# Moving work in the opening of a hash-attention and SwiGLU kernel: a turn, a bit copy, squares and zeros

## Chip, cores and metric

The kernel runs on one core of one Trainium2 chip. The metric is the device time of one execution in microseconds (us); the engines are named as the profile names them: PE (matmul; PEld is its weight load), DVE (vector), ACT (scalar), POOL (GpSimd) and SP (which here only issues DMAs).

## What is computed

First an attention with hashed buckets, over 4 batches, 8 heads, 768 tokens and a head size of 64; then a gated feed-forward layer on its output.

```python
q_bits = (einsum('bhsd,dk->bhsk', q, proj) > 0)        # 6 bits; k_bits likewise
mask = q_bucket[..., :, None] == k_bucket[..., None, :]
scores = where(mask, q @ k.T / 8, -1e9)
attn = softmax(scores);  x = (attn @ v)                 # [3072, 512] after the heads are joined
xn = x / sqrt(mean(x * x) + 1e-6) * rms_g
out = (silu(xn @ w_gate) * (xn @ w_val)) @ w_out        # 512 -> 1536 -> 512
```

## The kernel before

**The tiles.** A unit of work `w` is half a batch (384 queries), so there are eight. A pair `(b, hp)` is two heads of a batch. The six buffers `QK0` to `QK5` (line 95) each hold the turned keys and queries of one pair in fp16: rows 0 to 63 the 64 columns of the head, rows 64 to 75 twelve rows of hash bits, so that one matmul over the rows gives the score and a penalty for unequal bits. Pairs are given buffers in turn: (0,0) to (0,3) get QK0 to QK3, (1,0) and (1,1) get QK4 and QK5, (1,2) and (1,3) get QK0 and QK1 again. `score_rows` (line 141) says how many rows a score matmul reads: 76, or all 128 where rows 76 to 127 have been cleared by `clear_rows` (line 138), which the opening does on POOL for QK4 and QK5.

**The slots.** The program is written in a fixed order by hand. Each of the 192 slots (`SLOTS`, line 36) makes the scores of one head and a third of the keys (two PE matmuls of 384 columns, line 355) and one exponential on ACT (line 365). Score tiles have two buffers, so the scores of a slot wait for the exponential of two slots before. In slot `s` the scores of slot `s+1` are issued first; then the work planned for the slot with `at(s, f, ...)`, in order of rank, is issued to all engines. Every engine works its own queue in that order. So a wait of one instruction holds all that stands behind it on the same engine.

**From a load to a score in the first pairs.** SP loads a pair's `kL`, `qL`. PE turns a head (three transposes, line 181) into a bank `t_ps`; DVE copies it out to fp32 `kT` or `qT` (line 189); POOL, and ACT for a quarter, cast it into QK rows 0 to 63 (lines 195 and 197). A hash matmul on PE (line 221, bank `d_ps`) and a comparison on DVE (line 228) give `bits`. These lie on other partitions than the QK rows 64 to 75, so twelve rows at a time are moved: blocks 0 and 1 of each head by DVE copies (lines 261 and 281) and the odd blocks 2 and 3 by SP's DMA (lines 259 and 279). Slot 1 of a head of unit 0 reads block 2.

**After the scores.** `av` multiplies the exponentials with the values (line 377, one accumulator bank `o_ps`). DVE adds a small constant (`otmp`, line 392) and takes the reciprocal (397); POOL multiplies them into `x` (404) and makes its squares `sq` (416), and DVE sums these into `ssp` (420). For the pairs (0,2) and (0,3), which are called urgent, DVE does the product and squares with a running sum itself (404, 411). `norm` sums `ssp` to `ss` (427) and POOL makes `rstd` (429, 433). DVE scales `x` to `xn` (444), PE turns it (458, `x_ps`), DVE copies it to `xnT` (459), and the gate and value matmuls read that (473, 483). For unit 0 these turns stand in slots 38 to 40 and the first gate in slot 42. Until then PE has only attention work; afterwards each slot also holds products of the feed-forward layer.

**Idle products.** `idle` (line 345) issues matmuls of ones with ones whose result nobody reads: 28 and 5 in the opening, 8 ahead of the scores of slot 0 and 6 ahead of those of slot 3.

Of the kernel before, what the change touches and what calls it, by code (L numbers as in the profile page):

```python
# [48 lines left out]
def kernel(  # L49
# [33 lines left out]
    pk = const.tile([128, 48], FP32, name="pk")  # L83
    pq = const.tile([128, 48], FP32, name="pq")
    thr = const.tile([128, 1], FP32, name="thr")
    scl = const.tile([128, 1], FP32, name="scl")
    mhalf = const.tile([128, 3], FP32, name="mhalf")
    gcol = const.tile([128, 4], FP32, name="gcol")
# [46 lines left out]
        if (b, hp) not in QK:  # L135
            QK[b, hp] = qkbuf[len(QK) % len(qkbuf)]

    def clear_rows(i):
        nc.gpsimd.memset(qkbuf[i][D:128].rearrange("p h n -> p (h n)").bitcast(FP32), 0.0)

    def score_rows(b, hp):
        return slice(0, 128 if (b, hp) in ((1, 0), (1, 1)) or b > 1 else KROWS)

    def t_tile(b, hp, which):
        T0[b, hp, which] = tpool.tile(
# [119 lines left out]
    def hash_heads(b, hp):  # L265

        ps = hash_bank(
            [(w[:, 0:32], t0(b, 2 * hp + hh, which))
             for hh in range(2) for w, which in ((pk, "k"), (pq, "q"))]
        )  # L270
        bt = bits_tile(0)
        signs(bt, ps)

        def move(eng, blocks):
            for hh, t in blocks:
                p0 = 64 * hh + 32 * (t % 2) + 12 * (t // 2)
                dst, src = bit_rows(b, 2 * hp + hh, t), bt[p0 : p0 + 12]
                if eng is nc.sync:
                    eng.dma_start(out=dst, in_=src)
                else:  # L280
                    eng.tensor_copy(dst, src)

        return move

# [60 lines left out]
    def idle(ps, n):  # L345

        for _ in range(n):
            nc.tensor.matmul(ps, ones16, ones16, start=True, stop=True)  # L348

    def scores(g):  # L350
        w, h, p = SLOTS[g]
        ps = scps.tile([128, 2, 512], FP32, name="s_ps")
        idle(ps[:, 0, HALF:512], {0: 8, 3: 6}.get(g, 0))
        for j in range(2):
            nc.tensor.matmul(  # L355
                ps[:, j, 0:HALF], k_cols(w // 2, h, 2 * p + j), q_cols(w, h),
                start=True, stop=True,
            )
        sps[g] = ps
# [40 lines left out]
    def attn_x(w, hp, tmp, r):  # L400
        xd = x[w][:, :, 128 * hp : 128 * hp + 128]
        urgent = (w, hp) in ((0, 2), (0, 3))
        eng = nc.vector if urgent else nc.gpsimd
        eng.tensor_mul(  # L404
            xd.rearrange("p c (h d) -> p c h d", h=2), tmp[:, :, :, 0:64],
            r.to_broadcast([128, 3, 2, 64]),
        )
        sq = spool.tile([128, 3, 128], FP32, name="sq")
        if urgent:
            for c in range(3):  # L410
                nc.vector.scalar_tensor_tensor(
                    out=sq[:, c], in0=xd[:, c], scalar=1.0, in1=xd[:, c],
                    op0=ALU.mult, op1=ALU.mult, accum_out=ssp[w][:, c, hp : hp + 1],
                )
        else:
            nc.gpsimd.tensor_mul(sq, xd, xd)  # L416
        return sq

    def sumsq(w, hp, sq):
# [95 lines left out]
        load_rows(nc.sync, 0, hp, which)  # L515

    nc.vector.memset(ones16, 1.0)
    make_identity(nc, ident)
    nc.gpsimd.dma_start(out=pn[64:128], in_=proj)
    nc.vector.memset(pm, 0.0)  # L520
# [21 lines left out]
    for i in range(2):  # L542
        nc.gpsimd.memset(vls[i][:, :, :, 64:65], 1.0)
        nc.gpsimd.memset(vsum[i][:, :, 64:65], 6.0)
    clear_rows(4)
    clear_rows(5)

    def load_w(dst, src, n0, n1):
        nc.gpsimd.dma_start(
# [33 lines left out]
    keep(nc.scalar, 0, 0, "q")  # L583
    cast_half(0, 0, "q", 0, nc.scalar)
    columns_of_proj()
    idle(wz[:, 0:128], 5)
    bits0 = hash_head(0)
    keep(nc.scalar, 0, 1, "k")
# [18 lines left out]
    def at(s, f, *a, rank=3):  # L607
        plan[s].append((rank, len(plan[s]), lambda: f(*a)))
# [20 lines left out]
    for hp, turns, sv in ((1, (1, 2, 3, 5), 8), (2, (7, 8, 9, 10), 17), (3, (12, 13, 14, 15), 22)):  # L629
# [69 lines left out]
    for hp, s in enumerate((48, 62, 64, 78)):  # L699
        at(s, v_mean, 1, hp, 2)  # L700

    for i, s in ((2, 76), (3, 78), (0, 97), (1, 98)):
        at(s, clear_rows, i, rank=6)

    gts, sqs = {}, {}
# [5 lines left out]
        value(w, ft, gts.pop((w, ft)))  # L711

    def o_step(w, hp):
        sqs[w, hp] = attn_x(w, hp, *attn_out(w, hp))

    def o_first(w, hp):
        sqs[w, hp] = attn_out(w, hp)

    def o_last(w, hp):
        sqs[w, hp] = attn_x(w, hp, *sqs[w, hp])  # L720

    def s_step(w, hp):
        sumsq(w, hp, sqs.pop((w, hp)))
# [89 lines left out]
```

## Time and profile before

| what | value |
|---|---|
| median of 3 runs | 329.2 us (329.16 to 330.26) |
| the profiled execution's own time | 329.47 us |
| its span, first to last instruction | 327.6 us |
| PE, DVE, ACT, POOL busy | 321.5, 234.9, 208.1, 165.4 us |
| mean granted TensorE clock | 0.998 |
| HBM read, written | 28.58 MB, 6.29 MB |

The profile is one execution. Its span lies 1.9 us below its own time, and its own time 0.27 us above the median. A page of the profile gives busy times by engine and by source line, and views of the trace answer further: the waits (who waited for whom), the chain that ended last (followed back from the last instruction), the timeline (start, length, engine, line, operation; in brackets the idle time ahead and what ended it), and tables by stretches of time. A row "x6" is six instructions.

### The profile page before, as it was taken

To read this page: it belongs to the slowest core of one execution; us is meant where nothing else is said; L and a number is where in the kernel's file an instruction comes from. 1 tells how busy PE (TensorE), PEld (TensorE's weight loads), DVE (VectorE), ACT (ScalarE), POOL (GpSimd) and SP (SyncE) were. 2 spreads that over 40 slices of the span, in tenths; PEclk is the share of its full clock that TensorE was granted. 3 is DMA by queue.
4 is the path that set the end of the run, shared out by engine and by line. 5 is a ranking of instruction groups with operands and counts; after the bars stand their busy time and mean duration, and the time that the engine had idled before them with its cause. 6 is when DMAs were issued, how large, how long until landed. Compare 5 with 4: busy or idle time off the path is not lost.

```text
span 327.6 us, 7853 instructions
## 1 busy us (share of the span) xinstructions
PE 321.5 (98%) x2975; PEld 199.5 (61%) x2975; DVE 234.9 (72%) x526; ACT 208.1 (64%) x324; POOL 165.4 (50%) x238
## 2 busy tenths in 40 slices
PE   8998999999999999999999999999999999999995
PEld 7576766655566556655566656566566656655654
DVE  4798896888598976989487865967267824793860
ACT  3788986775576666657576766667677766423331
POOL 7887977278658685686734274733221320230000
PEclk9999999999999999999999999999999999999999
DMA  7998988984359729911470814001200012002002
GB/s 216 358 212 244 165 131 154 151 179 70 119 109 172 128 48 226 155 39 26 130 128 18 150 24 152 3 18 22 78 32 2 11 24 98 0 3 96 2 0 97
DMA packets 85509, 32.69 MB, mean 100 GB/s; under 512 B 70376, under 2 KB 82400, under 8 KB 85472
## 3 DMA queue, kind: packets, MB, share of 16 engines
q1 hardware_dynamic: 81392, 27.28, 35.2%
q0 software_dynamic: 3712, 4.72, 9.3%
q8 instruction: 23, 0.38, 0.5%
q10 hardware_dynamic: 368, 0.20, 0.2%
q14 instruction: 14, 0.11, 0.1%
HBM read 28.58 MB, written 6.29 MB: 106 GB/s over the span
## 4 chain that ended last, share of the span: by engine, by line
PE 94%; DMA 2%; ACT 2%; DVE 0%; issue 0%; DVEq 0%; ACTq 0%
PE v_ps L483 19%; PE s_ps L355 19%; PE y_ps L496 18%; PE g_ps L473 15%; PE o_ps L377 10%; PE d_ps L221 4%; PE s_ps L473 4%; PE t_ps L181 2%; DMA QK<-bits 2%; ACT psb L365 1%; PE z_ps L348 1%; PE x_ps L458 1%; DMA out_dram<-ysb 1%; PE m_ps L336 1%; DVE bits L228 0%
## 5 line engine op out<-in xcount | busy, mean ns | idle before, releaser
L365 ACT ACTIVATE psb<-s_ps 128x768 f16<-128x768 f32 x192 | 150.7, 809 | 30.1 <-PE s_ps L355 28.1
L355 PE MATMUL s_ps<-QK 128*128 128x384 f16 (+1 forms) x384 | 93.7, 326 | 1.3 <-DMA QK<-bits 0.5
L483 PE MATMUL v_ps<-xnT,wv 128*128 128x384 f16 x384 | 78.1, 326 | 0.0
L496 PE MATMUL y_ps<-wo,ht 128*128 128x512 f16 x276 | 69.2, 379 | 0.0
L404 POOL TENSOR_TENSOR x<-otmp,rcp 128x384 f32<-128x384 f32 x30 | 25.7, 857 | 83.4 <-DVE rcp L397 83.2
L377 PEld LDWEIGHTS <-psb 128*128 128x128 f16 x1152 | 51.7, 98 | 21.8 <-issue 3.7
L475 ACT ACTIVATE t<-g_ps 128x384 f32<-128x384 f32 x78 | 38.2, 490 | 40.7 <-PE g_ps L473 38.2
L473 PE MATMUL g_ps<-xnT,wg 128*128 128x384 f16 x312 | 63.5, 326 | 0.0
L484 DVE SCALAR_TENSOR_TENSOR t<-t,g_ps 128x384 f32<-128x384 f32 x78 | 42.9, 550 | 28.3 <-ACT t L475 28.2
L485 DVE SCALAR_TENSOR_TENSOR ht<-t,v_ps 128x384 f16<-128x384 f32 x96 | 53.2, 554 | 11.5 <-PE v_ps L483 1.0
L377 PE MATMUL o_ps<-vl,psb 128*128 128x65 f16 x1152 | 56.0, 193 | 0.0
L483 PEld LDWEIGHTS <-wv 128*128 128x128 f16 x384 | 36.5, 98 | 22.9
L473 PEld LDWEIGHTS <-wg 128*128 128x128 f16 x384 | 36.1, 98 | 23.0
L496 PEld LDWEIGHTS <-ht 128*128 128x128 f16 x276 | 26.3, 98 | 26.5 <-issue 2.1
L355 PEld LDWEIGHTS <-QK 128*128 128x128 f16 (+1 forms) x384 | 31.1, 97 | 16.8 <-issue 3.1
L503 ACT COPY ysb<-y_ps 128x512 f32<-128x512 f32 x23 | 13.5, 585 | 24.3 <-PE y_ps L496 23.7
L392 DVE TENSOR_TENSOR otmp<-o_ps,cvb 128x390 f32<-128x390 f32 x32 | 17.9, 559 | 14.9 <-PE o_ps L377 14.8
L416 POOL TENSOR_TENSOR sq<-x 128x384 f32<-128x384 f32 x30 | 25.5, 849 | 2.4
L213 POOL CAST QK<-kT 64x768 f16<-64x768 f32 x20 | 17.0, 848 | 10.8 <-DVE kT L205 8.9
L213 POOL CAST QK<-qT 64x768 f16<-64x768 f32 x20 | 16.5, 823 | 10.8 <-DVE qT L205 8.1
L205 DVE STREAM_TRANSPOSE kT<-kL 128x192 f32<-128x192 f32 x40 | 19.7, 521 | 0.0
L205 DVE STREAM_TRANSPOSE qT<-qL 128x192 f32<-128x192 f32 x40 | 19.4, 518 | 0.0
(81 smaller groups left out, 307.2 us busy)
## 6 DMA issues: line engine op xcount, KB each, us to landing
vL<-in_v_dram SPq DMA_DIRECT2D x16, 384.0 KB
out_dram<-ysb SPq DMA_DIRECT2D x23, 256.0 KB
kL<-in_k_dram SPq DMA_DIRECT2D x40, 96.0 KB
qL<-in_q_dram SPq DMA_DIRECT2D x40, 96.0 KB
kL<-in_k_dram SPq DMA_DIRECT2D x5, 384.0 KB
qL<-in_q_dram SPq DMA_DIRECT2D x5, 384.0 KB
wg<-in_moe_w_gate_dram POOLq DMA_DIRECT2D x2, 768.0 KB, 8.5
wv<-in_moe_w_val_dram POOLq DMA_DIRECT2D x2, 768.0 KB, 9.6
```

The costliest lines, as they stand in the source:

```text
L205: nc.vector.transpose(dst.rearrange("p (c t r) -> p r c t", c=6, r=4)[:, r : r + 1], src.rearrange("p (r c) d -> p r c d", r=4)[:, r : r + 1],
L213: nc.gpsimd.tensor_copy(QK[b, hp][0:64, hh, o : o + S], T0[b, hp, which][64 * hh : 64 * hh + 64, :])
L355: nc.tensor.matmul(ps[:, j, 0:HALF], k_cols(w // 2, h, 2 * p + j), q_cols(w, h), start=True, stop=True,)
L365: nc.scalar.activation(psb[w, h][:, p], sps.pop(g)[:, :, 0:HALF], AF.Exp, scale=ESCALE,)
L377: nc.tensor.matmul(o[:, c, hh, 0:65], psb[w, h][:, jt // 2, jt % 2, 128 * c : 128 * c + 128], vls[b % 2][:, h, v_chunk(b, h, jt), 0:65], s ...
L404: eng.tensor_mul(xd.rearrange("p c (h d) -> p c h d", h=2), tmp[:, :, :, 0:64], r.to_broadcast([128, 3, 2, 64]),)
L473: nc.tensor.matmul(g, wg[:, kt, fs], xnT[w][:, kt], start=(kt == 0), stop=(kt == 3))
L475: nc.scalar.activation(t, g, AF.Tanh, scale=0.5)
L483: nc.tensor.matmul(vv, wv[:, kt, fs], xnT[w][:, kt], start=(kt == 0), stop=(kt == 3))
L484: nc.vector.scalar_tensor_tensor(out=t, in0=t, scalar=1.0, in1=g, op0=ALU.add, op1=ALU.mult)
L485: nc.vector.scalar_tensor_tensor(out=ht[w][:, ft], in0=t, scalar=0.5, in1=vv, op0=ALU.mult, op1=ALU.mult)
L496: nc.tensor.matmul(y, ht[w][:, ft, c * 128 : (c + 1) * 128], wo[:, ft, :], start=(ft == 0), stop=(ft == NF - 1),)
```

## The change

1. The pair (0,1)'s second turn (head 2's queries) is planned in slot 1 instead of 2, and the six idle products ahead of slot 3 are left out. The cast that follows the turn moves with it.
2. The block 3 copies of heads 0 and 1 (DVE) move from slots 0 and 1 to slots 2 and 4, at the end of these slots.
3. For pair (0,2) the DVE copy of the second block of its first head moves from slot 14 to 13, and block 2 of that head is moved by a DMA that ACT issues, in slot 13, instead of the first of SP's four.
4. The squares of pair (0,0) and of unit 1's first pair on POOL are made in slots 22 and 25, apart from `x`, and their sums on DVE in slots 27 and 30. (They stood right behind `x`, with sums in slots 12 and 17.) In the urgent pairs each of the three squares on DVE now writes the one buffer of a tile `sqc`.
5. More zeros: QK1 and QK2 are cleared by POOL in the opening, QK4 by an ACT copy of a zero column, QK5 by DVE in two halves; QK0 is cleared by POOL in slot 50. The clears of QK2, QK0 and QK1 in slots 76, 97 and 98 go, the one of QK3 in slot 78 stays. All score matmuls but those of (0,0) and (0,3) then read 128 rows.

```diff
     def score_rows(b, hp):
-        return slice(0, 128 if (b, hp) in ((1, 0), (1, 1)) or b > 1 else KROWS)
+        return slice(0, KROWS if (b, hp) in ((0, 0), (0, 3)) else 128)
...
-        idle(ps[:, 0, HALF:512], {0: 8, 3: 6}.get(g, 0))
+        idle(ps[:, 0, HALF:512], {0: 8}.get(g, 0))
...
-                    out=sq[:, c], in0=xd[:, c], scalar=1.0, in1=xd[:, c],
+                    out=spool.tile([128, 128], FP32, name="sqc", bufs=1), in0=xd[:, c], scalar=1.0, in1=xd[:, c],
...
+    def attn_sq(w, hp):
+        xd = x[w][:, :, 128 * hp : 128 * hp + 128]
+        sq = spool.tile([128, 3, 128], FP32, name="sq")
+        nc.gpsimd.tensor_mul(sq, xd, xd)
         return sq
...
-    clear_rows(4)
-    clear_rows(5)
+    clear_rows(1)
+    clear_rows(2)
+    clear_rows(4, nc.scalar)
+    clear_rows(5, nc.vector, (0,))
...
     columns_of_proj()
+    clear_rows(5, nc.vector, (1,))
...
+        if (b, hp) == (0, 2):
+            odd = odd[1:]
...
-        at(h, (bits0, bits1)[h], (nc.vector,), 3)
+        at(2 + 2 * h, (bits0, bits1)[h], (nc.vector,), 3, rank=6)
...
-    for hp, turns, sv in ((1, (1, 2, 3, 5), 8), ...
+    for hp, turns, sv in ((1, (1, 1, 3, 5), 8), ...
...
-    for hp, s, slots in ((2, 12, (13, 14, 15, 16)), (3, 17, (18, 19, 20, 21))):
+    for hp, s, slots in ((2, 12, (13, 13, 15, 16)), (3, 17, (18, 19, 20, 21))):
...
+    at(13, lambda: moves[0, 2](nc.scalar, [(0, 2)]), rank=5)
...
-    for i, s in ((2, 76), (3, 78), (0, 97), (1, 98)):
+    for i, s in ((0, 50), (3, 78)):
         at(s, clear_rows, i, rank=6)
...
                 if (w, h) == (1, 1):
                     at(end, o_first, w, 0, rank=4.5)
                     at(end + 3, o_last, w, 0, rank=4.5)
+                    at(25, q_step, w, 0, rank=4.5)
+                    at(30, s_step, w, 0, rank=5)
                 else:
                     at(end, o_step, w, h // 2, rank=4.5)
-                if (w, h) not in ((0, 5), (0, 7)):
+                if (w, h) == (0, 1):
+                    at(22, q_step, w, 0, rank=4.5)
+                    at(27, s_step, w, 0, rank=5)
+                elif (w, h) not in ((0, 5), (0, 7), (1, 1)):
```

`q_step` calls `attn_sq`; `o_step` calls it too for all pairs but (0,0) and the urgent ones.

More of the change, by code (lines that the diff above doesn't have):

```diff
@@ L85 @@
     thr = const.tile([128, 1], FP32, name="thr")
+    zcol = const.tile([128, 1], FP32, name="zcol")
     scl = const.tile([128, 1], FP32, name="scl")
@@ L136, in qk_tile, with clear_rows @@
             QK[b, hp] = qkbuf[len(QK) % len(qkbuf)]
-    def clear_rows(i):
-        nc.gpsimd.memset(qkbuf[i][D:128].rearrange("p h n -> p (h n)").bitcast(FP32), 0.0)
+    def clear_rows(i, eng=nc.gpsimd, heads=(0, 1)):
+        for h in (heads if eng is nc.vector else (0,)):
+            part = qkbuf[i][D:128, h] if eng is nc.vector else (
+                qkbuf[i][D:128].rearrange("p h n -> p (h n)"))
+            part = part.bitcast(FP32)
+            if eng is nc.scalar:
+                eng.copy(part, zcol[D:128].to_broadcast([D, 2 * S]))
+            else:
+                eng.memset(part, 0.0)
     def score_rows(b, hp):
-        return slice(0, 128 if (b, hp) in ((1, 0), (1, 1)) or b > 1 else KROWS)
+        return slice(0, KROWS if (b, hp) in ((0, 0), (0, 3)) else 128)
     def t_tile(b, hp, which):
@@ L277, in move @@
                 dst, src = bit_rows(b, 2 * hp + hh, t), bt[p0 : p0 + 12]
-                if eng is nc.sync:
+                if eng is nc.vector:
+                    eng.tensor_copy(dst, src)
+                else:
                     eng.dma_start(out=dst, in_=src)
-                else:
-                    eng.tensor_copy(dst, src)
         return move
@@ L407, in attn_x @@
         )
-        sq = spool.tile([128, 3, 128], FP32, name="sq")
         if urgent:
@@ L517 @@
     nc.vector.memset(ones16, 1.0)
+    nc.vector.memset(zcol, 0.0)
     make_identity(nc, ident)
@@ L626 @@
         at(1 + h, cast_half, 0, h, "q", 1)
-        at(h, (bits0, bits1)[h], (nc.vector,), 3)
-    for hp, turns, sv in ((1, (1, 2, 3, 5), 8), (2, (7, 8, 9, 10), 17), (3, (12, 13, 14, 15), 22)):
+        at(2 + 2 * h, (bits0, bits1)[h], (nc.vector,), 3, rank=6)
+    for hp, turns, sv in ((1, (1, 1, 3, 5), 8), (2, (7, 8, 9, 10), 17), (3, (12, 13, 14, 15), 22)):
         for i, s in enumerate(turns):
@@ L713, in o_step @@
     def o_step(w, hp):
-        sqs[w, hp] = attn_x(w, hp, *attn_out(w, hp))
+        attn_x(w, hp, *attn_out(w, hp))
+        if (w, hp) not in ((0, 0), (0, 2), (0, 3)):
+            q_step(w, hp)
     def o_first(w, hp):
@@ L719, in o_last, with q_step @@
     def o_last(w, hp):
-        sqs[w, hp] = attn_x(w, hp, *sqs[w, hp])
+        attn_x(w, hp, *sqs.pop((w, hp)))
+    def q_step(w, hp):
+        sqs[w, hp] = attn_sq(w, hp)
     def s_step(w, hp):
```

2 lines of the change are left out of this document (removed).

## The prediction

> **What bounds the kernel now.** First the head of the page.
>
> ```profile
> span 327.6 us, 7853 instructions
> ```
> ```profile
> PE 321.5 (98%) x2975; PEld 199.5 (61%) x2975; DVE 234.9 (72%) x526; ACT 208.1 (64%) x324; POOL 165.4 (50%) x238
> ```
>
> PE is busy in all but 6.1 us of the span, so the first question is where those 6.1 us are. A table by stretches of 8 us answers it from one side:
>
> ```profile
> 40.00:48.00 8.00, 7.86 (x99) 4.80 (x97) 7.83 (x22) 6.83 (x10) 5.90 (x11) 1.00 0.94 151
> 48.00:56.00 8.00, 8.00 (x80) 5.23 (x79) 5.65 (x12) 5.76 (x10) 6.05 (x10) 1.00 0.92 160
> ```
>
> (Columns: stretch, length, busy PE, PEld, DVE, ACT, POOL, granted clock, DMA share, GB/s.) From 48 us on PE is full at a clock of 1.00. The first gate matmul stands there. From then on a microsecond lost or won earlier is carried to the end, and work on other engines costs nothing while PE is fed. So only the first 49 us count, and they end with the start of the gate. The waits of PE in the first 52 us:
>
> ```profile
> PE s_ps L355 <- DMA QK<-bits: 0.5, 1, 0.5
> PE s_ps L355 <- ACT psb L365: 0.3, 1, 0.3
> PE s_ps L348 <- ACT psb L365: 0.2, 1, 0.2
> PE s_ps L355 <- ACT qT L189: 0.2, 1, 0.2
> PE s_ps L355 <- DVE QK L281: 0.2, 1, 0.2
> ```
>
> They are few and short, 1.4 us together. The chain that ended last, followed in this window, shows two more things:
>
> ```profile
> 10.97 0.50 PE s_ps L348 x6
> ...
> 13.17 1.00 PE d_ps L221 x8
> ...
> 16.81 0.78 PE d_ps L221 x8
> ...
> 23.48 5.21 DMA QK<-bits
> 28.69 0.14 issue
> 28.83 0.34 PE s_ps L355
> ```
>
> The six idle products stand on the chain; a hash takes 0.78 us when fed and 1.00 us when its operands come late; and the score at 28.83 us had waited for a bit transfer handed to SP's queue 5.21 us before.
>
> **The change, part by part.** The order of the changed program's instructions is known, its times are not; what follows sets rows of this trace into that order.
>
> *Opening zeros: nothing.* QK4's clear becomes one ACT copy of 64x1536, for which there is no row. The nearest:
>
> ```profile
> L365 ACT ACTIVATE psb<-s_ps 128x768 f16<-128x768 f32 x192 | 150.7, 809 | 30.1 <-PE s_ps L355 28.1 <-PE m_ps L336 0.8
> ```
> ```profile
> L503 ACT COPY ysb<-y_ps 128x512 f32<-128x512 f32 x23 | 13.5, 585 | 24.3 <-PE y_ps L496 23.7
> ```
>
> 256 more elements cost 0.22 us, so 1536 would take 809 + 3 x 224 = 1.48 us; bounds 0.59 and, at twice my value, 3.0. It lies in this gap of ACT, of which it uses half, and its cover is gone only at the upper bound:
>
> ```profile
> 5.54 0.48 ACT L189 COPY qT<-t_ps 128x384 f32<-128x384 f32 x1 [2.94 <-PE t_ps L181]
> ```
>
> QK5's two halves, 64x768 on DVE, lie between the 165 ns and half of the 1372 ns of these rows (as they stand; up to all of it if DVE is slower than POOL); I take 0.69 us.
>
> ```profile
> L517 DVE MEMSET ones<- 128x128 f16 x1 | 0.2, 165 | 0.8 <-PEq L797 0.8
> ```
> ```profile
> L139 POOL MEMSET QK<- 64x1536 f32 x6 | 8.2, 1372 | 0.3
> ```
>
> One falls into each of two gaps of DVE, 1.40 and 1.34 us. Only at the upper bound would the second be full, for 0.1 us.
>
> ```profile
> 4.90 0.56 DVE L189 COPY kT<-t_ps 128x384 f32<-128x384 f32 x1 [1.40 <-PE t_ps L181]
> ```
> ```profile
> 6.98 0.68 DVE L228 TENSOR_SCALAR bits<-d_ps,thr,scl 128x384 f16<-128x384 f32 x1 [1.34 <-PE d_ps L221]
> ```
>
> POOL clears two buffers there as before. Fewer clears later are worth nothing, as PE is full there. Reading 128 rows instead of 76 costs and gains nothing in a score matmul:
>
> ```profile
> L355 PE MATMUL s_ps<-QK 128*128 128x384 f16 x240 | 58.7, 326 | 0.0
> ```
> ```profile
> L355 PE MATMUL s_ps<-QK 76*128 76x384 f16 x144 | 35.0, 325 | 1.3 <-DMA QK<-bits 0.5 <-ACT psb L365 0.3 <-ACT qT L189 0.2
> ```
>
> *Idle products and the earlier turn: a lead of about 0.6 us by 14 us.* The turn now fills the wait for ACT ahead of slot 3, and the six products go: 0.50 us of the chain. ACT takes some of it, as its exponentials 3 to 5 run back to back. On DVE two of the four bit copies ahead of head 2's keys and queries go, so the hash at 13.17 no longer waits: 1.00 - 0.78 = 0.22. I take 0.6; bounds 0.2 (the hash alone) and 0.72.
>
> *The moved copies come back on DVE* between 12 and 16 us, where it has a little idle time, and its queue then runs without a break to the hash of pair (0,2). The lead is kept, not enlarged: 0.6.
>
> *Pair (0,2): the lead grows to about 1.4 us at 29 us.* Two things stood there. One is the sum at 23.37 on DVE, which goes:
>
> ```profile
> L420 DVE TENSOR_REDUCE ssp<-sq 128x3 f32<-128x384 f32 x30 | 16.0, 532 | 0.9 <-POOL sq L416 0.8
> ```
>
> With it go about 0.5 us from the queue ahead of the next hash, and the wait of 0.2 for a DVE bit copy, which now stands ahead of a turn's copy instead of behind it. The other is the bit transfer. SP's timeline:
>
> ```profile
> 19.26 0.46 SPq L117 DMA_DIRECT2D kL<-in_k_dram  x1
> 19.82 0.41 SPq L117 DMA_DIRECT2D qL<-in_q_dram  x1
> 23.48 3.53 SPq L279 DMA_DIRECT2D QK<-bits  x4
> ```
>
> The block that the score waits for was the first of the four, and the two loads of `kL` and `qL` stood in the same queue ahead of it. On ACT's queue nothing does. It stands there behind one exponential, needs the comparison (which moves with the lead), and holds the next exponential for the time of its issue. The trace has one issue from ACT:
>
> ```profile
> 0.74 0.55 ACTq L510 DMA_DIRECT2D pn<-in_proj_dram  x1
> ```
>
> So 0 to 0.88 us (SP's 3.53 / 4) of ACT's sequencer, mostly while ACT is still at the exponential before it: I take 0.3. The landing is not shown; it may come anywhere from 1 us after the issue to the old 5.2. I take some 3 us, about 26 us, ahead of the score, which with the lead is due near 27. Then the waits of 0.5 and 0.3 go as well: 0.6 + 0.5 + 0.2 + 0.5 - 0.3 is 1.5, less what SP's next four transfers, for (0,3), may hold: 1.4. Bounds 0 (it lands as before) and 1.9 (no issue cost, and the 0.3 for ACT too).
>
> *The squares moved back: 1.25 us of the lead is spent.* The two sums now stand on DVE between `otmp` of (0,2) at 35.5 and `otmp` of (0,3), which is the road to the gate: 2 x 0.53 = 1.06 us. There the three squares of an urgent pair also change. Now they start 0.22 us apart, shorter than one lasts:
>
> ```profile
> 41.63 0.29 DVE L411 SCALAR_TENSOR_TENSOR sq<-x 128x128 f32<-128x128 f32 x1
> 41.85 0.08 DVE L411 DVE_READ_ACCUMULATOR sq<-x 128x1 f32 x1
> 41.85 0.29 DVE L411 SCALAR_TENSOR_TENSOR sq<-x 128x128 f32<-128x128 f32 x1
> ```
>
> After the change all three write one buffer, and the second and third each wait for the one before: about 0.1 us each, four times, 0.4 (bounds 0 and 0.8). Together 1.5. There is one gap to hide it in:
>
> ```profile
> 39.67 0.56 DVE L189 COPY qT<-t_ps 128x384 f32<-128x384 f32 x1 [0.29 <-PE t_ps L181]
> ```
>
> That leaves 1.2 to 1.25. POOL now makes both squares in the same stretch; its gap ahead of the norm is about as long as two of them,
>
> ```profile
> 42.74 0.19 POOL L429 TENSOR_SCALAR ms<-ss 128x3 f32<-128x3 f32 x1 [1.56 <-DVE ss L427]
> ```
>
> so the norm need not wait for POOL, but the second sum may, by 0.2. So of 1.4 us about 0.15 is left when `ss` is ready. Behind it all is one chain: POOL's `rstd`, DVE's `xn`, PE's turns, DVE's `xnT`, the gate.
>
> ```profile
> 47.26 1.25 DVE L459 TENSOR_TENSOR xnT<-x_ps,gcol 128x512 f16<-128x512 f16 x2
> ```
> ```profile
> 48.72 0.81 PE L473 MATMUL g_ps<-xnT,wg 128*128 128x384 f16 x4
> ```
>
> Now `xnT` is ready at 48.51 and PE comes to the gate at 48.72: 0.2 us of slack that the lead may also use. The gate starts about 0.3 us earlier, and PE waits out the rest of its lead at the turns of `xn`.
>
> *Sum.* Zeros 0; lead 1.4; spent 1.25; slack used 0.15 to 0.2; net -0.3 us. Against the profiled execution 329.47 - 0.3 = 329.2; that execution is 0.27 above the median of 329.2, so the forecast for the median is **328.9 us**, a change of 0.1%. About 0.5%, or 1.65 us, is what a measurement of this kernel can tell from no change: below 327.55 is faster, above 330.85 slower.
>
> **The rivals.**
>
> *The lead arrives whole.* If the sums find gaps on DVE, or the queue reaches them before the pairs' other work, the gate moves by the lead itself, 1.1 to 1.9 us: 327.3 to 328.1, say 327.8. For it: the gap at 39.67 shows that DVE is not full before it, only fed late by PE. Against it: 7.83 busy of 8 us in the stretch from 40 to 48.
>
> *The sums cost more than the lead: slower.* The place is DVE's queue from 35.5 us to `ss`, the price 1.25 us less 0.2 of slack, and it decides as soon as the lead at 35.5 us is under about 1.05. If the bits land on ACT's queue no sooner than they did on SP's, the score at 28.83 us stays where it is, the lead there is 0, and the gate comes 1.05 us later: 330.3. With a lead of 0.5 it is 329.7. For it: the landing is the least known term, and no row shows a bit transfer that was quick. Against it: the queue ahead of the old one held two loads. This is also the case in which the change doesn't do what it says. The Trainium skill's page "DMA: Bandwidth & Descriptors", in "Issuing engines are not separate DMA queues", says that transfers run on the same 16 engines whoever issues them, and that a second issuer saves only issue time. By that rule this rival is the likely one; the trace has no bit transfer on ACT's queue to weigh it.
>
> *The clock falls back.* Six products go and turns take their place; if the granted clock halved for a stretch like the one before the first warm work,
>
> ```profile
> 1.05 3.17 PE z_ps L348 x28
> ```
>
> PE's work of 3.17 us would need twice that: up to 3.2 us more on a road that has little slack, 331 to 332.5, say 331.3. Against it: PE's gaps there get shorter, and the clock stays at 1.00 through the present waits. The Trainium skill's page "TensorE: Matmul & The Clock Gate", section "Part 4: PE-mode transpose", says that turns do not count as busy for the clock, which speaks against just this exchange; in this trace turns and scores alternate and the clock stays up.
>
> **How the numbers follow.** Forecast (328.5 to 329.4): 0.47. Lead whole: 0.26, of which nearly half below 327.55. Slower by the sums: 0.22, of which 0.05 above 330.85. Clock: 0.05. That gives faster 0.12, same 0.78, slower 0.10. The range leaves out 0.1 at each side: it cuts the lead-whole case at 327.5 and takes in the sums' 330.3: 327.5 to 330.4.
>
> **What would show each step.** Right: no wait at the six products' place, the hash at 13 us lasting 0.78; no wait for a bit transfer near 28 us; the score now at 28.83 starting near 27.4; then a new wait of PE on `xn` (line 444 in the old numbering) or on `xnT` ahead of the gate, about 1 us. Wrong: PE waits for `bits` from ACT's queue; ACT idle by the length of an issue; no wait at the turns of `xn` and a gate 1 us or more earlier; a granted clock under 1.00 after 8 us; DVE gaps around the two moved sums.

## The result, and the profile after

| kernel | median us (range, runs) | ratio to before, 95% interval |
|---|---|---|
| before | 329.36 (329.16 to 330.26, 5) | |
| changed | 331.83 (331.70 to 332.70, 5) | 1.0077 (1.0059 to 1.0094) |

The change is slower by 2.5 us; the forecast was 328.9. The profiled execution of the changed kernel took 331.81 us (before 329.47), its span is 330.0 us. First the same table of stretches for both, before and then changed (stretch, length, busy PE, PEld, DVE, ACT, POOL, clock, DMA share, GB/s):

```profile
24.00:28.00 4.00, 3.85 (x53) 2.56 (x52) 3.73 (x11) 3.67 (x7) 3.54 (x8) 1.00 0.77 224
28.00:32.00 4.00, 3.23 (x42) 2.38 (x39) 3.07 (x6) 3.03 (x5) 2.85 (x4) 1.00 0.92 293
44.00:48.00 4.00, 3.93 (x57) 2.55 (x56) 3.97 (x9) 3.49 (x5) 3.70 (x6) 1.00 0.69 103
sum 56.00, PE 53.42 PEld 37.54 DVE 44.09 ACT 42.99 POOL 45.20; mean PE 6.68 PEld 4.69 DVE 5.51 ACT 5.37 POOL 5.65
```
```profile
24.00:28.00 4.00, 3.12 (x45) 2.31 (x45) 3.73 (x10) 2.64 (x5) 2.87 (x7) 1.00 0.92 244
28.00:32.00 4.00, 3.48 (x47) 2.15 (x47) 1.69 (x4) 3.50 (x6) 2.21 (x3) 1.00 0.98 312
44.00:48.00 4.00, 2.49 (x40) 1.58 (x37) 3.90 (x13) 2.96 (x4) 2.56 (x6) 1.00 0.70 114
sum 56.00, PE 51.39 PEld 35.07 DVE 44.67 ACT 42.65 POOL 43.58; mean PE 6.42 PEld 4.38 DVE 5.58 ACT 5.33 POOL 5.45
```

In the first 56 us PE stands idle 56 - 53.42 = 2.58 us before and 4.61 us after. So 2.03 of the 2.34 us between the two profiled executions are idle time of PE here, in two places: 0.73 us more from 24 to 28 (0.25 of it comes back from 28 to 32) and 1.44 us more from 44 to 48. PE's waits in the changed kernel name both:

```profile
PE s_ps L363 <- ACT psb L373: 1.5, 3, 0.9
PE x_ps L468 <- DVE xn L454: 1.1, 1, 1.1
```

The first comes from ACT's timeline. The transfer that ACT issues occupies it for 1.57 us, and the next exponential starts at 25.69 instead of 24.19:

```profile
23.52 0.81 ACT L373 ACTIVATE psb<-s_ps 128x768 f16<-128x768 f32 x1 [0.51 <-PE s_ps L363]
24.02 1.57 ACTq L289 DMA_DIRECT2D QK<-bits  x1
25.69 1.51 ACT L373 ACTIVATE psb<-s_ps 128x768 f16<-128x768 f32 x2 [1.36 <-PE t_ps L189]
```

The second is the end of a long row on DVE, from the squares of pair (0,2) to `ss`:

```profile
37.83 0.80 DVE L418 SCALAR_TENSOR_TENSOR sqc<-x 128x128 f32<-128x128 f32 x1
...
38.67 0.49 DVE L418 SCALAR_TENSOR_TENSOR sqc<-x 128x128 f32<-128x128 f32 x1
...
39.20 0.29 DVE L418 SCALAR_TENSOR_TENSOR sqc<-x 128x128 f32<-128x128 f32 x1
...
39.42 0.55 DVE L197 COPY qT<-t_ps 128x384 f32<-128x384 f32 x1
39.89 0.55 DVE L430 TENSOR_REDUCE ssp<-sq 128x3 f32<-128x384 f32 x1
...
41.36 0.55 DVE L430 TENSOR_REDUCE ssp<-sq 128x3 f32<-128x384 f32 x1 [0.26 <-POOL sq L426]
41.83 0.55 DVE L197 COPY qT<-t_ps 128x384 f32<-128x384 f32 x1
42.29 0.55 DVE L400 TENSOR_TENSOR otmp<-o_ps,cvb 128x390 f32<-128x390 f32 x1
...
44.89 0.17 DVE L437 TENSOR_REDUCE ss<-ssp 128x3 f32<-128x12 f32 x1
```

The same row before:

```profile
35.53 0.56 DVE L392 TENSOR_TENSOR otmp<-o_ps,cvb 128x390 f32<-128x390 f32 x1 [0.35 <-PE o_ps L377]
...
37.23 0.29 DVE L411 SCALAR_TENSOR_TENSOR sq<-x 128x128 f32<-128x128 f32 x1
...
37.45 0.29 DVE L411 SCALAR_TENSOR_TENSOR sq<-x 128x128 f32<-128x128 f32 x1
...
37.66 0.58 DVE L411 SCALAR_TENSOR_TENSOR sq<-x 128x128 f32<-128x128 f32 x1
...
40.15 0.55 DVE L392 TENSOR_TENSOR otmp<-o_ps,cvb 128x390 f32<-128x390 f32 x1
...
42.39 0.17 DVE L427 TENSOR_REDUCE ss<-ssp 128x3 f32<-128x12 f32 x1
```

The first `otmp` of (0,2) stands at 36.22 (35.53 before), the second, of (0,3), at 42.29 (40.15). So the way between the two grew by 6.07 - 4.62 = 1.45 us: two more sums, and three squares that last 0.80, 0.49 and 0.29 and start 0.84 and 0.53 us apart. The wait for POOL adds little, since the row had a wait of 0.29 us at about the same place before (for PE, at 39.67). The gate follows 2.47 us late (48.72 before; the chain of waits has both 0.16 later, and the expectations below count to those):

```profile
51.19 0.81 PE L483 MATMUL g_ps<-xnT,wg 128*128 128x384 f16 x4
```

### The profile page after: what moved, and what is told of

Same layout as the page of the kernel before. It is cut to its first block, busy times and chain, and to the rows that moved or that the text cites. A ratio compares the mean times of both kernels' runs of the same rounds, so it can differ in the third digit from the quotient of the medians.

```text
span 330.0 us, 7840 instructions
## 1 busy us (share of the span) xinstructions
PE 321.7 (97%) x2969; PEld 198.7 (60%) x2969; DVE 236.7 (72%) x529; ACT 209.4 (63%) x325; POOL 163.2 (49%) x236
## 3 DMA queue, kind: packets, MB, share of 16 engines
q1 hardware_dynamic: 81368, 27.27, 35.5%
## 4 chain that ended last, share of the span: by engine, by line
PE 90%; DVE 5%; POOL 1%; ACT 1%; issue 1%; DMA 1%; DVEq 0%; POOLq 0%; ACTq 0%
PE v_ps L493 19%; PE y_ps L506 18%; PE s_ps L363 17%; PE g_ps L483 15%; PE o_ps L385 10%; PE d_ps L229 4%; PE s_ps L483 4%; PE t_ps L189 1%; PE z_ps L356 1%; PE x_ps L468 1%; DVE qT L197 1%; DVE sqc L418 1%; ACT psb L373 1%; DVE bits L236 1%; DVE xn L454 1%
```

## The experiments

The theory after this profile (S): DVE's row from `otmp` of (0,2) to `xn` ends last, through the moved sums and the trio's shared tile. Rivals: ACT's 1.57 us go through to the gate (H), or the opening does it, since the first exponential came at 9.30 us and not at 8.89 (O). Medians, each with its ratio to the runs of before on the same chip (329.28 to 329.51 us). What the texts call ScalarE, VectorE and GpSimd are ACT, DVE and POOL, and the pair (1,0) of the sums is unit 1's first pair. In e2 and e5 the texts name (0,1) among the moved squares by mistake: only those of (0,0) and of unit 1's first pair are moved.

| run | what it is | median us | ratio, 95% interval |
|---|---|---|---|
| e1 | changed, block 2 on SP's queue | 331.31 | 1.0061 (1.0049 to 1.0074) |
| e2 | changed, squares, sums, tile back | 330.37 | 1.0031 (1.0019 to 1.0043) |
| e3 | changed, two buffers for `sqc` | 331.26 | 1.0062 (1.0049 to 1.0075) |
| e4 | changed, e1 and e2 together | 329.73 | 1.0010 (1.0001 to 1.0018) |
| e5 | before, squares and sums moved | 333.35 | 1.0105 (1.0082 to 1.0128) |
| e6 | before, block 2 by ACT | 329.51 | 1.0008 (0.9994 to 1.0023) |
| e7 | before, the turn and the two copies | 329.49 | 1.0003 (0.9993 to 1.0014) |
| e8 | before, the turn alone | 329.62 | 1.0003 (0.9994 to 1.0012) |
| e9 | changed, sum of unit 1's pair back | 330.58 | 1.0031 (1.0019 to 1.0043) |
| e10 | changed, sum of (0,0) back | 330.18 | 1.0017 (1.0003 to 1.0030) |
| e11 | e5 with two buffers for `sqc` | 331.32 | 1.0045 (1.0026 to 1.0064) |
| e12 | before, weights loaded later | 330.19 | 1.0023 (1.0008 to 1.0039) |
| e13 | changed, later turns of (1,1) | 332.05 | 1.0075 (1.0059 to 1.0091) |
| e14 | before, later turns of (1,1) | 330.43 | 1.0029 (1.0018 to 1.0040) |
| e15 | e1 and e10 and e13 together | 330.19 | 1.0022 (1.0012 to 1.0032) |

**e1.**
```diff
-        if (b, hp) == (0, 2):
-            odd = odd[1:]
...
-    at(13, lambda: moves[0, 2](nc.scalar, [(0, 2)]), rank=5)
```


> The changed kernel with one part undone: block 2 of pair (0,2)'s bits goes back to SP's queue, as the first of four transfers there; the rest of the change stays. Theory H (ScalarE held by its own transfer): in the changed kernel ScalarE was in the transfer's issue from 24.02 to 25.59 us and the next exponential began at 25.69 instead of 24.19, while the block landed at about 29.4, no sooner than before. Without it that exponential should begin near 24.2 to 24.5, the first otmp of pair (0,2) should move from 36.22 to 35.4 to 35.7, and the gate, still behind the longer row on VectorE, from 51.35 to about 50.2 to 50.8: 330.6 to 331.3 us. Theory S (the sums and the squares on VectorE's queue are nearly all of it, and the lag at 36 us is swallowed): no change, 331.7 to 331.9. Theory O (the opening, 0.41 us late at the first scores, carries through to the gate): no change from this edit either, 331.6 to 331.9, with otmp still near 36.1.

The exponential is back at 24.40, as H said, but `otmp` of (0,2) comes at 36.08 and PE is idle from 44 to 48 as in the changed kernel:

```profile
28.00:32.00 4.00, 2.75 (x40) 2.05 (x38) 2.12 (x4) 2.67 (x5) 2.08 (x3) 1.00 0.90 290
44.00:48.00 4.00, 2.54 (x35) 1.52 (x32) 3.90 (x13) 2.76 (x4) 2.66 (x5) 1.00 0.89 138
```

What ACT gave back, PE then waited for the same block of bits: idle 1.25 us from 28 to 32, where the changed kernel has 0.52. Its score went on at 29.39, 5.55 us after the end of the comparison; in the changed kernel it was 29.53, 5.58 after. (The trace names POOL's `x` for this wait, since it has no landing there; in e12 the same score started 1.2 us before that `x` had ended, so it doesn't wait for it.) So the profile speaks against H as the cause of the loss at the gate. The median doesn't decide: it is 0.5 us lower than that of the changed kernel, at the upper end of H's range and below S's, with intervals that overlap.

**e2.**
```diff
-                    out=spool.tile([128, 128], FP32, name="sqc", bufs=1), in0=xd[:, c], ...
+                    out=sq[:, c], in0=xd[:, c], ...
...
-        if (w, hp) not in ((0, 0), (0, 2), (0, 3)):
+        if (w, hp) not in ((0, 2), (0, 3)):
             q_step(w, hp)
...
         attn_x(w, hp, *sqs.pop((w, hp)))
+        q_step(w, hp)
...
-                    at(22, q_step, w, 0, rank=4.5)
-                    at(27, s_step, w, 0, rank=5)
...
-                    at(25, q_step, w, 0, rank=4.5)
-                    at(30, s_step, w, 0, rank=5)
```


> The changed kernel with the squares and sums of pairs (0,0), (0,1) and (1,0) back where they stood, and the three squares of (0,2) and (0,3) into one tile of three slices as before; the transfer on ScalarE's queue stays. Theory H+S (both count): the row on VectorE from otmp of (0,2) to the gate falls from 15.13 us (36.22 to 51.35) to about the 13.35 of before (35.53 to 48.88), and the lag of 0.7 us at 36.22 stays or grows a little by the sum that returns at 23.4: gate 49.5 to 50.2, 330.0 to 330.7 us. Theory S alone: 329.3 to 329.7. Theory H alone (all from ScalarE's stall): 331.4 to 331.9. Theory O: the 0.41 us of the opening remain in any case, 329.8 or more.

1.46 us came back. From the start of `otmp` of (0,2) to the end of the last `xnT` DVE took 49.23 - 36.30 = 12.93 us, as before (48.51 - 35.53 = 12.98) and not the 14.78 of the changed kernel (51.00 - 36.22). This run has ACT's transfer on its chain, from issue to landing:

```profile
23.97 5.51 DMA QK<-bits
29.48 0.14 issue
29.62 0.34 PE s_ps L363
```

**e3.**
```diff
-                    out=spool.tile([128, 128], FP32, name="sqc", bufs=1), ...
+                    out=spool.tile([128, 128], FP32, name="sqc", bufs=2), ...
```


> The changed kernel with one size changed: the tile sqc that the three squares of a trio share gets two buffers instead of one, so a square no longer writes where the one before it wrote. In the changed kernel the trios took 1.59 us (37.83 to 39.42) and 1.15 (43.70 to 44.84) against 0.95 and 0.68 before. Theory W (the shared buffer makes each square wait for the one before): the squares of the second trio start 0.21 to 0.25 us apart again, and it is 0.3 to 0.45 us shorter; what the first trio gains is lost at the second sum, which waits for GpSimd's squares until 41.32. Time 331.3 to 331.6. Rival (GpSimd's multiply beside them slows the squares, not the shared buffer): the trios keep their length, 331.7 to 331.9.

Theory W holds for the second trio, whose squares start 0.22 us apart again and not 0.33:

```profile
44.46 0.29 DVE L418 SCALAR_TENSOR_TENSOR sqc<-x 128x128 f32<-128x128 f32 x1
44.68 0.08 DVE L418 DVE_READ_ACCUMULATOR sqc<-x 128x1 f32 x1
44.68 0.29 DVE L418 SCALAR_TENSOR_TENSOR sqc<-x 128x128 f32<-128x128 f32 x1
```

The first trio stays slow (0.47, 0.58 and 0.62 us, and 1.20 for the `x` ahead of it, 0.75 in the changed kernel), so there something else stretches these instructions. POOL's square was under way beside that `x` (37.81 to 38.64), and all the profiles fit with POOL: of their 102 such squares, the 44 with no POOL instruction beside them took 0.28 or 0.29 us, and all 33 that took 0.47 or more had one beside them; but so had 25 short ones. e10 below comes nearest to a test. In the second trio, too, the first square is 0.29 us here with nothing on POOL beside it and 0.48 in the changed kernel with a cast beside it, so the tile's buffers are worth about half of the 0.42 us by which this trio is shorter. The time is 0.6 us lower with overlapping intervals.

**e4.** The diffs of e1 and e2 together.


> The changed kernel with both undone: block 2 on SP's queue, squares and sums where they stood. What stays of the change is the second turn of pair 1 for the idle products, the two bit copies later, the copy of pair (0,2) in slot 13 and the zeros. Theory H+S: nothing of the 2.47 us at the gate is left but what the opening and the rest bring; the lag of 0.41 at the first scores was made good by 14 us in the changed kernel, so 328.9 to 329.6 us, near the 329.4 of before. Theory O (the opening's lag or the zeros carry through): 329.8 to 330.4 or more. Theory T (what I forecast: the turn and the early copy give a lead of their own once nothing holds ScalarE): 328.3 to 329.0.

The median lies between the range of H+S and that of O. O as a fixed lag of 0.41 us falls, as this execution has the first exponential at 8.88. In fact that start differs from run to run: 8.59 to 9.71 us over the nine profiles with the changed opening, 8.63 to 9.28 over the eight with that of before; whether the changed opening is later on average stays open. Theory T falls: the lead of 0.43 us at 14.5 us is there, and all but 0.09 of it gone by the comparison of (0,2). What remains is 0.1%, near the bound of what is resolved.

**e5.** The reverse of e2's diff, on the kernel before, with the tile `sqc` of one buffer.


> The kernel before with one part of the change: the squares and sums of pairs (0,0), (0,1) and (1,0) moved back, and the trios of (0,2) and (0,3) into the one shared tile. Nothing holds ScalarE and nothing of the opening differs. Theory S (moving them is nearly the whole loss by itself: two sums, a wait for GpSimd's late square, and stretched operations on VectorE between the first otmp of (0,2) and the gate, 15.13 us there against 13.35): that row again 14.9 to 15.3 us, 330.7 to 331.2 us. Rival (the sums cost only because ScalarE's hold had already made the pair late, so that alone they fit into VectorE's waits): the row at 13.4 to 14.0, 329.3 to 330.0 us.

Slower than the whole change, and outside both theories. The profiled execution (336.14 us) had one long wait for bits of (0,3), and a low clock behind it:

```profile
PE s_ps L363 <- DMA QK<-bits: 4.7, 1, 4.7
```
```profile
32.00:40.00 8.00, 3.29 (x39) 2.41 (x38) 2.25 (x8) 2.60 (x5) 5.58 (x9) 0.73 1.10 183
40.00:44.00 4.00, 4.00 (x46) 3.15 (x44) 2.70 (x9) 3.28 (x5) 2.56 (x4) 0.68 1.17 198
```

All four executions had a mean clock of 0.988 to 0.995, where the slowest of before on this chip (330.86) had 0.998. So this run shows that the squares alone lose time, not how much the row costs; e11 was made for that.

**e6.** The block of (0,2) by ACT, alone on the kernel before (the reverse of e1's diff).


> The kernel before with one part of the change: block 2 of pair (0,2)'s bits by a transfer on ScalarE's queue, the other three on SP's. With the block back on SP's queue in the run before (e1), PE went on at 29.4 us as in the changed kernel, 5.5 us after the end of the signs; so theory L (the landing, 5.4 to 5.7 us after the signs on either queue, covers ScalarE's hold of 1.5 us): the stall shows, the next exponential 1.0 to 1.5 us later than the 24.19 of before, but the first otmp of (0,2) stays within 0.3 us of 35.5 and the time is 329.1 to 329.8 us. Theory H (the hold goes through to the gate): 330.0 to 330.6 us.

L holds in the time. In the profiled execution, one of the longer ones (330.49), the stall shows and part of it goes through: the next exponential at 25.18, `otmp` of (0,2) at 36.10, which L had within 0.3 us of 35.5.

```profile
23.48 1.60 ACTq L289 DMA_DIRECT2D QK<-bits  x1
25.19 1.51 ACT L373 ACTIVATE psb<-s_ps 128x768 f16<-128x768 f32 x2 [1.17 <-PE s_ps L363]
```

**e7, e8.** On the kernel before; e8 without the last two lines.
```diff
-        idle(ps[:, 0, HALF:512], {0: 8, 3: 6}.get(g, 0))
+        idle(ps[:, 0, HALF:512], {0: 8}.get(g, 0))
...
-    for hp, turns, sv in ((1, (1, 2, 3, 5), 8), ...
+    for hp, turns, sv in ((1, (1, 1, 3, 5), 8), ...
...
-        at(h, (bits0, bits1)[h], (nc.vector,), 3)
+        at(2 + 2 * h, (bits0, bits1)[h], (nc.vector,), 3, rank=6)
```


> The kernel before with one part of the change: pair 1's second turn in place of the six idle products, and the two copies of bits moved from steps 0 and 1 to 2 and 4. In the run with bits and squares back (e4) the exponentials were 0.43 us ahead of before at 14.5 us (14.48 against 14.91) and the signs of pair (0,2) only 0.09 ahead (22.68 against 22.77), after a copy of bits at 17.93 that took 0.67 us where the one at 18.44 of before took 0.25. Theory C (the copies moved back lie on VectorE's busy row and eat the lead): lead of 0.4 us at 14 us, 0 to 0.15 at the signs, 329.0 to 329.5 us. Rival (the lead carries through, and e4 lost it by the copy put into step 13 instead): 328.6 to 329.0 us.

> As the run before it (e7), but the two copies of bits stay at steps 0 and 1: the second turn replaces the idle products and nothing is added to VectorE's row after 14 us. Theory C: the lead of about 0.4 us lasts to the signs of pair (0,2) (22.3 to 22.5 instead of 22.77), their block lands that much sooner, PE goes on at 28.4 to 28.5 instead of 28.83, and the time falls to 328.7 to 329.0 us. Rival (VectorE's row after 14 us is as full with the copies early, since the turns and signs wait for PE and GpSimd anyway): 329.1 to 329.5 us, as e7. If the copies at steps 0 and 1 now hold VectorE while the new turn waits to be copied, there is no lead at 14 us at all, and 329.2 to 329.6.

In e7 the lead, counted from the first exponential, is 0.42 us at the seventh (14.88 - 9.28 against 14.91 - 8.89) and 0.09 at the comparison of (0,2) (23.08 - 9.28 against 22.78 - 8.89), the numbers of theory C. In e8 there is none at the seventh at all (14.91, as before), which was its third case. So the lead came only with the moved copies, and neither gave any time. The place where it is lost can be seen in the changed kernel and in before. Changed, then before:

```profile
17.65 0.68 DVE L236 TENSOR_SCALAR bits<-d_ps,thr,scl 128x384 f16<-128x384 f32 x1
18.35 0.67 DVE L269 COPY QK<-bits 12x384 f16<-12x384 f16 x1
19.05 0.56 DVE L197 COPY qT<-t_ps 128x384 f32<-128x384 f32 x1
```
```profile
17.74 0.68 DVE L228 TENSOR_SCALAR bits<-d_ps,thr,scl 128x384 f16<-128x384 f32 x1
18.45 0.25 DVE L261 COPY QK<-bits 12x384 f16<-12x384 f16 x1
18.73 0.56 DVE L189 COPY qT<-t_ps 128x384 f32<-128x384 f32 x1
```

Counted from the first exponential (9.30 and 8.89), the comparison at 17.65 still leads by 0.50 us, behind both moved copies, and the `qT` at 19.05 by 0.09. So it isn't the room that the moved copies take, as theory C had it, but the one copy between, which takes 0.67 us instead of 0.25. It takes 0.66 to 0.68 in all the runs with the moved copies, 0.25 in before, e6 and e8, but 0.57 in e12 too, where nothing was moved ahead of it. In the changed kernel POOL's cast of `vl` ran beside it for 0.55 us, in before for 0.11; that this is the cause was not tested.

**e9, e10.** On the changed kernel, of e2's diff only the part of unit 1's first pair (the lines with 25 and 30, and `q_step` behind `attn_x`), or only that of (0,0) (the lines with 22 and 27, and the condition).


> The changed kernel with one thing undone: the square of pair (1,0) and its sum go back to where they stood (right behind x, sum three or four slots later); pair (0,0)'s stay moved, the shared tile and ScalarE's transfer stay. In the changed kernel this sum waited on VectorE for GpSimd's square (41.10 to 41.36) and held the copy behind it until 41.83; the products after xn then came late, and PE was idle 1.51 us between 44 and 48 us. Theory S (VectorE's row ends last): the row from otmp of (0,2) to the gate falls from 15.13 us by 0.7 to 0.9, and with it the time, 330.8 to 331.2 us. Rival H (PE's lag at 36 us sets the gate as well): 331.5 to 331.9.

> The changed kernel with the other one undone: pair (0,0)'s square and sum back, (1,0)'s stay moved. Theory S: 0.46 us go (39.89 to 40.35 on VectorE), but the sum of (1,0) still waits for its square, which GpSimd makes up to 0.8 us sooner with one square less ahead of it: 0.4 to 0.9 us, 330.9 to 331.4 us. Rival (the wait for GpSimd alone decides, and the sum of (0,0) lies in its shadow): 331.5 to 331.9. Together with e9 and e3 this says how the 1.46 us that e2 gave back divide.

Either gives back half of the loss or more, 1.25 and 1.65 us of 2.5, more than was expected of either, and together more than the 1.46 of e2. On DVE's row the parts do add up: from `otmp` of (0,2) to `ss` it takes 8.67 us in the changed kernel, 7.78 in e9, 7.62 in e10 and 6.81 in e2 (6.86 before). Why e10, with one sum still moved, is no slower than e2 stays open. e10 takes back more than its sum: POOL's square of (0,0) no longer runs beside the first square of (0,2), which is 0.29 us instead of 0.80, and the trio lasts 1.06 us (37.35 to 38.41) instead of 1.59. That first square took 0.80 in all five profiles with POOL's square beside it (changed, e1, e9, e11, e13), and 0.29 in e10 and e15 without it. PE's idle time from 44 to 48 us is 0.70 and 0.71 us instead of 1.51:

```profile
44.00:48.00 4.00, 3.30 (x42) 2.06 (x38) 4.00 (x7) 3.54 (x6) 3.58 (x7) 1.00 0.86 137
```
```profile
44.00:48.00 4.00, 3.29 (x42) 2.12 (x45) 4.00 (x8) 3.58 (x6) 3.85 (x6) 1.00 0.63 93
```

**e11.** The kernel of e5 with e3's diff.


> The kernel before with the squares and sums moved as in the run e5, but two buffers for the tile of the trio. e5 was 3.5 us slower than before, 1 us more than the whole change; in its profile PE waited 4.7 us for a transfer of bits of pair (0,3) and was granted 0.50 of its clock in the stretch from 36 to 40 us. Theory M (chance of a transfer, that can come again or not, on top of a loss of 1.4 to 1.9 us): without the late transfer the time is 330.6 to 331.2 us. Rival (moving the squares makes the transfers of (0,3) late every time, since the loads are issued in another order against them): the wait of 3 to 5 us shows again, 332 to 335 us.

The long wait did not come again in the profiled execution, and the wait for `xn` is the 1.1 us of the changed kernel, with nothing on ACT's queue:

```profile
PE x_ps L468 <- DVE xn L454: 1.1, 1, 1.1
```

Of the ten times four are 330.4 to 330.5, four 331.3 to 331.4 and two 333.3 and 333.4. M gave 330.6 to 331.2, between the first two groups. The profiled one (333.25) is of the last; in it the clock was 0.80 behind the wait for `xn`, where PE had stood idle for 1.22 us:

```profile
44.00:48.00 4.00, 2.78 (x40) 1.69 (x37) 3.97 (x13) 2.89 (x4) 2.81 (x7) 0.97 0.95 146
48.00:56.00 8.00, 8.00 (x74) 4.59 (x73) 5.50 (x11) 4.80 (x8) 5.99 (x10) 0.80 0.81 140
```

8 us at 0.80 and 4 at 0.97 are 1.7 us, about the distance of the last group from the second (1.9). A mean clock of 0.995, as in these two, also stood in three of the four executions of e5 (0.994 to 0.995), so the clock may be part of what e5 lost beyond this run. But one of the executions of e11 at 331.3 had 0.994 as well, so clock and groups don't match one to one; why it fell in all four of e5 stays open.

**e12.**
```diff
-        at(2 + 4 * i, load_w, t, src, 0, 768)
-        at(19 + 5 * i, load_w, t, src, 768, 1536)
+        at((2, 19)[i], load_w, t, src, 0, 768)
+        at((24, 33)[i], load_w, t, src, 768, 1536)
```


> Not a part of the change: the kernel before with the first load of wv (768 KB) put where the second of wg stood, and each later half one place on. In every run so far, on SP's queue or ScalarE's, block 2 of pair (0,2) landed 5.4 to 5.7 us after its signs ended, and PE waited 0.47 us for it in before; 768 KB of wg, 768 of wv and 768 of keys and queries are under way until 26 to 27 us. Theory Q (the landing is set by what is under way, not by the queue it is handed to): with 768 KB less the block lands 1 us or more sooner, the wait of 0.47 us goes, the first otmp of (0,2) comes at 35.0 to 35.2 instead of 35.52, and the time is 328.7 to 329.1 us, below both kernels. Rival (the landing is the price of the transfer itself): otmp stays at 35.4 to 35.6 and the time at 329.2 to 329.6; if the weights then come too late for the gate, 329.8 or more.

The landing is as Q said, the gain is not. The DMA engines' share from 24 to 28 us is 0.08 instead of 0.77, and the score no longer waits for bits: it starts at 28.39, 4.59 us after the end of its comparison, which itself came 0.34 us late, behind that copy of 0.57 us. PE has a new wait of 0.4 us for an `otmp`, and the time rises by 0.7 us; PE waits for no weights in this profile, and what the rise comes from stays open. So what else is under way sets part of the landing; it didn't make a kernel that beats the two.

**e13, e14, e15.** The turns of (1,1), on the changed kernel, on the kernel before, and on the changed one with the diff of e1 and the (0,0) part of e2's.
```diff
-        (1, (13, 14, 36), (29, 31, 33, 35), 40, (45, 47), (49, 51)),
+        (1, (13, 14, 36), (29, 33, 35, 37), 40, (45, 47), (49, 51)),
```


> The whole changed kernel, and one thing of its own: the second, third and fourth turn of pair (1,1) go from steps 31, 33 and 35 to 33, 35 and 37. That takes one copy (qT, 41.83 to 42.29 in the changed kernel) out of VectorE's row ahead of the last otmp, to behind ss, and the last of three copies there to behind xn; every square and sum stays where the change put it. Theory S (the row's length ends last): xn comes 0.4 to 0.5 us sooner, PE's idle time of 1.51 us between 44 and 48 us falls by as much, 331.2 to 331.5 us against the 331.8 of the changed kernel. Rival (the wait for GpSimd's squares and its order decide): 331.7 to 332.0.

> The same step in the kernel before, where PE is busy 4.00, 3.93 and 3.93 of each 4 us from 36 to 48 us. Theory S: xn comes 0.4 us sooner, but PE has other work until the gate either way, so no more than the 0.14 us idle there can come back: 329.1 to 329.6 us. Rival (the gate waits for xn in the kernel before too): 328.8 to 329.1 us.

> The changed kernel with block 2 back on SP's queue and pair (0,0)'s square and sum back where they stood; (1,0)'s stay moved, and the later turns of e13 are added. e10 (the sum alone) gave 330.2, e1 showed that ScalarE's transfer matters only where VectorE's row isn't the last to end; here it has 0.46 us less. Theory S: the row no longer ends last, PE's idle time before the gate is that of e4 or less, 329.3 to 329.8 us. If the lead of the second turn (0.43 us at 14 us) now comes through, 328.7 to 329.1, below both kernels; if PE still waits for xn, 330.0 or more.

In e13 the wait for `xn` falls from 1.1 to 0.4 us and PE's idle time from 44 to 48 us from 1.51 to 1.00, as S expected, but 0.27 and 0.31 us of idle time are new from 40 to 44 and from 48 to 56, with one of the copies now ahead of `xnT`; the time (332.05) is not in S's range. It takes one step of S out of its place and puts another in it, so it doesn't decide between the theories. In e14 nothing was gained, as S said, but 0.95 us lost, which none of the texts foresaw; its cause is open. e15, at 330.19, is in the range of its last case, below the changed kernel but not below the one before. No run here beats the kernel before.

## Why the prediction was wrong

**The opening zeros: right in size.** ACT's clear took 1.47 us (forecast 1.48) and DVE's two 0.70 each (0.69), in their gaps. That they cost no time was not tested alone; e4 has them within its 0.1%.

```profile
2.64 1.47 ACT L145 COPY QK<-zcol 64x1536 f32<-64x1536 f32 x1
```
```profile
3.69 0.70 DVE L147 MEMSET QK<- 64x768 f32 x1 [0.20 <-issue]
...
5.85 0.70 DVE L147 MEMSET QK<- 64x768 f32 x1 [0.22 <-issue]
```

**The turn, a lead of 0.6 us by 14 us: right in kind.** From the first exponential to the seventh it is 5.60 against 6.02 us in the changed kernel, e4 and e7, a lead of 0.42. The hash at 13.37 took 0.78 us, as forecast.

**"The lead is kept": the first step that failed.** It is used up on DVE's row before the comparison of (0,2): 13.97 us behind the first exponential, 13.89 before. Not the moved copies use it up but the copy at 18.35, which lasted 0.42 us longer than the one of before; the forecast had no term for a copy that lasts longer. e7 shows the loss alone.

**Pair (0,2), "the lead grows to about 1.4 us at 29 us": the step that decided.** Measured is no lead but a lag of 0.69 at `otmp` of (0,2). Of it 0.41 is the later first exponential of this execution; counted from there 0.28 is left (26.92 us against 26.64). It is 0.27 in e1 and e4 (26.91), where ACT issues nothing.

The term that failed is the landing. I took 3 us, and the one landing of bits in the rows of before took 5.21. The block lands no sooner by ACT's queue than by SP's: 5.51, 5.74 and 5.92 us after its issue in e2, e10 and e9, against 5.18 to 5.62 in before, e5, e7, e8 and e15. The forecast of 3 us rested on the two loads ahead of it in SP's queue, which have no part in this: e1 put the block back behind them, and the score went on 20.22 us after the first exponential (20.23 in the changed kernel). The rule that I cited from the Trainium skill, "DMA: Bandwidth & Descriptors", section "Issuing engines are not separate DMA queues", gave this rival; these runs agree with it on the landing (5.51 against 5.21 us), and e12, where fewer bytes were under way, points the same way.

ACT's hold was mis-sized too: 1.57 us, where I took 0.3 and 0.88 at most. What it costs in time is small or nothing alone (e6), 0.5 us with overlapping intervals between the changed kernel and e1, and 0.6 us between e2 and e4.

**The squares, "1.25 us of the lead is spent": too small.** The row from `otmp` of (0,2) to the gate grew by 1.78 us (51.19 - 36.22 against 48.72 - 35.53). The sums were sized about right (0.46 to 0.47 each between starts) and the wait for POOL too (0.26 for 0.2). The squares were not: 37.83 to 39.42 and 43.70 to 44.89 are 1.59 and 1.19 us, against 0.94 and 0.76 before (37.23 to 38.17, 41.63 to 42.39), 1.08 more for both; I took 0.4, with an upper bound of 0.8. The shared buffer alone was sized right: starts 0.33 instead of 0.22 us apart, four times 0.11. The other 0.6 is that single squares last longer, which I had put at nothing; most of it lies in the first trio, where one took 0.80 beside the square on POOL that the change itself had moved there (e10). The 0.2 us of slack at the gate wasn't used: `xnT` ends 0.19 us ahead of it (51.00), 0.21 before.

**So the slower rival came true, at a higher price.** "The sums cost more than the lead" named this place and this condition. With no lead it gave 1.05 us and 330.3. What came was 0.41 us of a late start, a lag of 0.28 and 1.78 us on the row: 2.47 at the gate. How much of the medians' 2.5 is the start isn't known, since it varies from run to run. That the lead was missing shows in e1, e4 and e7; that the sums alone are a loss, in e5 and e11; that taking either away ends half of it or more, in e9 and e10. One of the signs that I had listed for being right came all the same, a new wait of PE on `xn` of 1.1 us; but it came because DVE's row was late, not because PE was early.

**The clock falls back: not in the changed kernel's profile,** where it is 1.00 throughout, but behind PE's idle time in e5 and e11, with the half clock that I had assumed (0.50 from 48 to 51 us in e11).

## What to carry to other kernels

Before a transfer is moved to another engine's queue, ask what ends its landing: here it came 5.2 to 5.9 us after it was handed over, from whichever queue, and the issue held the engine for twice what SP needs for one. A piece of work is free only where the queue that it enters has room; the two sums were moved onto the one row that ends at the gate, and the square that moved with them ran beside that row's own squares, one of which took 0.80 us instead of 0.29. And with two waits in one kernel, the earlier one can be mended with little gain (0.5 us in e1) until the last one is.

## What the runs showed of the hardware

- The issue of one transfer of 12 rows of 768 bytes held ACT for 1.55 to 1.60 us (e2, the changed kernel, e6); SP's four took 3.53 us together.
- A square with a running sum that writes the buffer of the one before it starts 0.33 us after it at best; with two buffers 0.22 us, although each lasts 0.29.
- DVE squares of 128x128 took 0.28 or 0.29 us whenever POOL had nothing beside them (44 of 102), and up to 0.80 beside a POOL instruction; the one of 0.80 was 0.29 again when POOL's square was taken away from there (e10, e15).
- The same DVE copy of 12x384 took 0.25 us in some runs and 0.67 in others, and a product of 128x384 0.56 to 1.20; that POOL is the cause there too was not tested.
- The mean granted clock was 0.80 over the 8 us (0.50 in the first 3) after PE had been idle 1.22 us of 4 in e11, and stayed at 1.00 after 1.51 of 4 in the changed kernel.
